# Five V tiles of a decode attention kernel are loaded by four transfers each instead of one

## The chip, the core and the metric

The kernel runs on one core of a Trainium2 chip. The metric is the device time of one execution in microseconds (us). A core has a TensorE (PE) for matrix products, a VectorE (DVE), a ScalarE (ACT), a GpSimd (POOL), and a SyncE (SP), which here does nothing but wait and issue transfers. Sixteen DMA engines move the data from HBM into the on-chip memory, which has 128 partitions (rows).

## What is computed

Four attention layers in a row, each for a single query token: layers 0 and 2 use the weights and caches A, layers 1 and 3 use B. Each layer has 32 heads of 192 dimensions and a cache of 8192 positions, so that every layer reads 32 x 8192 x 192 bf16 values of K and as many of V (about 100 MB each) and does very little arithmetic on each.

```python
q = (layernorm(x) @ wq).reshape(32 heads, 192)
scores = einsum("hd,hkd->hk", q, k_cache) * 192 ** -0.5
p = softmax(scores)
o = einsum("hk,hkd->hd", p, v_cache)
x = x + o.reshape(1, 32 * 192) @ wo
...
x = x + A(x); x = x + B(x); x = x + A(x); x = x + B(x)
```

## The kernel before

**Tiles.** A layer works on 16 pairs of heads. The K cache of a pair, and its V cache, is one tile of 128 partitions by 24576 bf16 values, 49152 bytes in each partition, 6144 KB in all: partitions 0 to 63 hold the first head, 64 to 127 the second, and one partition holds 128 positions of 192 values. Half a tile is TS = 12288 values a partition. The on-chip buffer `pool` has NSLOT = 8 half-tile slots, so that four whole tiles fit at a time.

**Work on a pair.** `products` (line 600) has DVE multiply the K tile in place with the query; PE then adds up over the dimensions by matrix products with an identity (lines 613 and 58) into the score banks S. `softmax` makes the weights p_sb (line 637). `values` (lines 679 and 58) has PE multiply p_sb with the V tile into OY, and `gather` (lines 703, 705, 717) puts the parts together. After five pairs, `project` (line 537) applies a third of the output weights.

**The order of the loads.** The list `plan` holds all loads in the order in which SP issues them: the query weights, then K and V of one pair after another, with the three parts of the output weights between. `allot` gives every load its slots and notes in `before` which earlier holders of these slots must be done. `ahead` issues from the list as long as the release of those holders is already known in the program; in `transfer` SP waits for these events (`*free`) and then issues the load. SP issues in order, so a load that waits for its slot holds back all later ones.

**How a load is issued.** `whole(kind, l, p)` tells whether a tile comes by one transfer. Then `transfer` issues one transfer of 128 partitions for both halves (line 378), and the request for the second half gives back the same event. The other tiles come as two halves (line 380). Every transfer adds 16 to the semaphore semS[i] of its first slot when it has landed, and the event that `SP.op` gives back is the count after it, so that whoever waits for the event waits for all transfers issued on that semaphore so far.

```python
if whole(*n[:3]):
    if n[3] == 1:
        return landed[n[:3] + (0,)]
    f = lambda s: s.dma_start(pool[:, i * TS:(i + 2) * TS], r)
```

Here n is (kind, layer, pair, half), and r is the pair's cache in HBM as 128 rows of 24576 values.

Of the kernel before, what the change touches and what calls it, by code (L numbers as in the profile page):

```python
# [63 lines left out]
PAIRS_W = 5  # L64
NSLOT = 8
KEPT = {0: {("k", 0)}, 1: {("v", 14), ("v", 15)}}


def build(nc, A_x, A_k, A_v, A_wq, A_wo, B_x, B_k, B_v, B_wq, B_wo, out):
    _, H, SK, DH = A_k.shape  # L70
    D = A_x.shape[-1]
    P = 128
# [12 lines left out]
    TS = JU * DH  # L85
# [11 lines left out]
    with ExitStack() as ctx:  # L97
        def sb(name, shape, dt):
            return ctx.enter_context(nc.sbuf_tensor(name, shape, dt))
# [4 lines left out]
        def sem(name):  # L104
            return ctx.enter_context(nc.semaphore(name))

        ident = sb("ident", [P, P], BF16)
        pool = sb("pool", [P, NSLOT * TS], BF16)
# [61 lines left out]
        SP = Queue()  # L170
        semS = [sem(f"semS{i}") for i in range(NSLOT)]
        semOL, semOE, semOB, semVQ, semX, semOUT = [sem(n) for n in ("semOL", "semOE", "semOB", "semVQ", "semX", "semOUT")]

        e = PO.op(lambda g: g.memset(ident[:], 0.0))
# [6 lines left out]
        e = PO.op(lambda g: g.memset(mask, 0.0))  # L181
        for t in range(G):
            e = PO.op(lambda g, t=t: g.affine_select(
                out=mask, in_=mask, compare_op=ALU.not_equal, fill=1.0,
                base=-32 * t, pattern=[[-1, 2], [-2, VK]], channel_multiplier=1), e)
# [10 lines left out]
        def pair(l, p):  # L196
            return ORDER[l]["pairs"][p]

        def first_load(kind, l, p):

            n = (kind, pair(l, p))
            if l >= 2 and n in KEPT[l - 2]:
                return (l - 2, ORDER[l - 2]["pairs"].index(n[1]))
            return (l, p)

        def stays(kind, l, p):
            return l < 2 and (kind, pair(l, p)) in KEPT[l]

        def whole(kind, l, p):

            if kind == "t":
                return False
            if kind == "k":
                return l < 2 and p not in (PAIRS_W, 2 * PAIRS_W) or l == 3 and p > 1
            if p == NPAIR - 1:
                return False
            return l != 2 or p not in (0, PAIRS_W, 2 * PAIRS_W)
# [7 lines left out]
        for l in range(NL):  # L225
# [8 lines left out]
            for p in range(NPAIR):  # L234
# [17 lines left out]
                if p < NPAIR - 2:  # L252
                    if first_load("v", l, p) == (l, p):
                        plan += [("v", l, p, u) for u in range(2)]
                        if l == 2 and p == 1:
                            i = plan.index(("k", l, 1, 0))
# [76 lines left out]
        def wq_rows(l, g):  # L333

            c0, k = Q_PARTS[g]
            if l < 2:
                i = place[("wq", l, 0)] * TS
                return pool[:, i + c0 * QW:i + (c0 + k) * QW].rearrange("p (c n) -> p c n", c=k)
            return slot[place[("wq", l, g)]][:, 0:k * QC].rearrange("p (c n) -> p c n", c=k)

        def quarters(n):
            return n[0] == "v" and n[2:] == (NPAIR - 1, 1) and NB[n[1]] > 0

        def transfer(n):
            l = n[1]
            o = ORDER[l]
            w = W[l % 2]
            free = [freed[b] for b in before[n]]
            if n[0] in ("wol", "woe"):
                r0 = o["wol"] * PD  # L350
                a, b = (0, OI) if l < 3 else (0, OI - 1) if n[0] == "wol" else (OI - 1, OI)
                return SP.op(lambda s: s.dma_start(
                    rows[:, a * D:b * D], w["wo"][r0:r0 + PD].rearrange("(p i) n -> p (i n)", p=P)[:, a * D:b * D]),
                    *free, sem=semOL if n[0] == "wol" else semOE, inc=16)
            if n[0] == "t":
                return max(free, key=lambda e: e[1]) if free else None
            if n[0] == "wob":
                r0 = o["wo"][2] * PD
                return SP.op(lambda s: s.dma_start(
                    slot[place[("wo", l, 2)]][:, (NW - NB[l]) * D:NW * D],  # L360
                    w["wo"][r0:r0 + PAIRS_W * PD].rearrange("(p i) n -> p (i n)", p=P)[:, (NW - NB[l]) * D:]),
                    sem=semOB, inc=16)
            if n[0] == "vq":
                n = ("v", l, NPAIR - 1, 1)
            i = place[n]
            t = slot[i]
            if n[0] in "kv":
                h = 2 * pair(l, n[2])
                r = w[n[0]][0, h:h + 2].rearrange("h (p j) d -> (h p) (j d)", j=J)
                if quarters(n):  # L370
                    x = TS // 2
                    if n in landed:
                        return SP.op(lambda s: s.dma_start(t[:, x:], r[:, TS + x:]), sem=semVQ, inc=16)
                    return SP.op(lambda s: s.dma_start(t[:, 0:x], r[:, TS:TS + x]), *free, sem=semS[i], inc=16)
                if whole(*n[:3]):
                    if n[3] == 1:
                        return landed[n[:3] + (0,)]
                    f = lambda s: s.dma_start(pool[:, i * TS:(i + 2) * TS], r)
                else:
                    f = lambda s: s.dma_start(t, r[:, n[3] * TS:(n[3] + 1) * TS])  # L380
            elif n[0] == "wq" and l < 2:
                f = lambda s: s.dma_start(pool[:, i * TS:i * TS + DC * QW], w["wq"].rearrange("(p c) n -> p (c n)", c=DC))
            elif n[0] == "wq":
                c0, k = Q_PARTS[n[2]]
                f = lambda s: s.dma_start(
                    wq_rows(l, n[2]),
                    w["wq"][:, o["q1"] * PD:o["q1"] * PD + QC].rearrange("(p c) n -> p c n", c=DC)[:, c0:c0 + k, :])
            else:
                r0 = o["wo"][n[2]] * PD
                k = NW - NB[l] if n[2] == 2 else NW  # L390
                f = lambda s: s.dma_start(
                    t[:, 0:k * D], w["wo"][r0:r0 + PAIRS_W * PD].rearrange("(p i) n -> p (i n)", p=P)[:, 0:k * D])
            return SP.op(f, *free, sem=semS[i], inc=16)

        def need(n):

            while n not in landed:
                m = plan[issued[0]]
                issued[0] += 1
                landed[m] = transfer(m)  # L400
            return landed[n]

        def ahead():

            while issued[0] < len(plan):
                m = plan[issued[0]]
                if any(b not in freed for b in before[m]):
                    return
                issued[0] += 1
                landed[m] = transfer(m)  # L410
# [373 lines left out]
        e = SP.op(lambda s: s.dma_start(out[0, 0].rearrange("(h n) -> h n", h=2), ev_z[0:33:32, :]), ev_true, sem=semOUT, inc=16)  # L784
# [54 lines left out]
```

## Time and profile before

| | |
|---|---|
| median of 3 runs | 1981.34 us (1981.29 to 1982.41) |
| profiled execution, its own time | 1981.74 us |
| its span, first to last instruction | 1979.9 us |
| busy share PE, DVE, ACT | 65%, 61%, 7% |
| moved by the DMA engines | 849.22 MB, mean 429 GB/s over the span |
| transfers of whole V tiles of cache A | 27, 6144 KB each, median 26.7 us from issue to landing |
| instruction packets on queue q8 | 45, 0.74 MB |

The profile is one execution. Its second part cuts the span into 40 equal slices: a digit is the busy share in tenths, the line "DMA" is the mean share of the sixteen DMA engines, and the line "GB/s" what they moved. The third part lists the DMA queues: q1 is what SP issues, q8 and q14 bring instructions to the engines. The fourth part is the chain of waits that ended last, followed back from the end. The sixth part lists transfers by line with their size and the median time from issue to landing. Beside the page, the trace can be asked for the busy times of a stretch, for the waits of an engine, for the pieces of the chain in order of time, and it holds the time of each of the sixteen completions of every transfer (though not which DMA engine sent it) and of each packet.

### The profile page before, as it was taken

Reading aid. Unit: us, or ns where it says so; the run is one execution under the profiler, and the core shown is the slowest. Engines: PE = TensorE matmul, PEld = TensorE weight load, DVE = VectorE, ACT = ScalarE, POOL = GpSimd, SP = SyncE. Lnnn points to the kernel's source line nnn. Section 1 sums busy time; section 2 is a strip of 40 time slices with the busy share of each in tenths; the row PEclk is TensorE's granted clock in tenths of the full one; section 3 lists DMA queues with packets and bytes.
Section 4 is the critical chain, followed back from the end, with each engine's and each line's share of the span. In section 5 each row is a group of like instructions: output and inputs, shape, how many; then the busy total and the mean of one; then the engine's idle time right before and its main releaser. Section 6 shows DMA issues by size and latency. Waiting matters only on the chain.

```text
span 1979.9 us, 13244 instructions
## 1 busy us (share of the span) xinstructions
PE 1285.2 (65%) x8248; PEld 146.3 (7%) x3160; DVE 1202.0 (61%) x872; ACT 139.8 (7%) x462; POOL 4.5 (0%) x23
## 2 busy tenths in 40 slices
PE   3567566666466666665785676675676767656668
PEld 0001001000200100000020010010001001000001
DVE  3567467467166656556755565665764765655756
ACT  0000000000000000000010000000000100000000
POOL 0000000000000000000000000000000000000000
PEclk9777776778587777777887877878877778777779
DMA  9999999999999999999999999999999999999998
GB/s 413 431 435 431 432 430 431 434 435 425 434 435 431 430 432 432 430 436 430 427 409 435 426 428 430 430 430 432 431 427 427 436 431 430 435 432 433 430 432 372
DMA packets 26927, 849.22 MB, mean 429 GB/s; under 512 B 3059, under 2 KB 3189, under 8 KB 3829
## 3 DMA queue, kind: packets, MB, share of 16 engines
q1 hardware_dynamic: 26724, 848.38, 99.7%
q8 instruction: 45, 0.74, 0.2%
q14 instruction: 14, 0.11, 0.0%
q10 hardware_dynamic: 144, 0.00, 0.0%
HBM read 848.36 MB, written 0.00 MB: 428 GB/s over the span
## 4 chain that ended last, share of the span: by engine, by line
DMA 61%; PE 23%; DVE 13%; ACT 1%; issue 1%; SPq 0%
DMA pool<-in_B_k_cache_dram 24%; DMA pool<-in_A_v_cache_dram 19%; DMA pool<-in_A_k_cache_dram 14%; PE S L58 13%; DVE pool L600 10%; PE OY L58 5%; DMA pool<-in_B_v_cache_dram 4%; PE OY L679 3%; ACT p_sb L637 1%; DVE OY L703 1%; DVE s_sb L622 1%; PE S L613 1%; DVE acc L705 1%; PE OY L537 1%; DVE m_bf L624 0%
## 5 line engine op out<-in xcount | busy, mean ns | idle before, releaser
L600 DVE TENSOR_TENSOR pool<-pool,q_sb 128x3072 bf16<-128x3072 bf16 (+1 forms) x368 | 851.0, 2378 | 191.2 <-DMA pool<-in_B_k_cache_dram 106.5
L58 PE MATMUL S<-pool,ident 128*128 128x512 bf16 x2944 | 784.0, 426 | 15.5 <-DVE pool L600 14.5
L703 DVE TENSOR_TENSOR OY<-OY,small 128x1536 f32<-128x1536 f32 x60 | 106.0, 1766 | 250.6 <-PE OY L58 250.5
L717 PE MATMUL TB<-acc,small 128*1 128x192 f32 x240 | 82.9, 496 | 210.2 <-DVE acc L705 210.2
L613 PE MATMUL S<-pool,ident 128*128 128x512 bf16 x128 | 62.1, 485 | 216.5 <-DVE pool L600 216.3
L58 PE MATMUL OY<-pool,p_sb 128*16 128x512 bf16 x1920 | 200.0, 493 | 0.0
L679 PE MATMUL OY<-pool,p_sb 128*16 128x512 bf16 (+1 forms) x1216 | 147.3, 493 | 61.2 <-DMA pool<-in_A_v_cache_dram 57.7
L622 DVE TENSOR_REDUCE s_sb<-S 128x64 f32<-128x512 f32 x128 | 87.8, 686 | 126.1 <-PE S L58 126.0
L705 DVE TENSOR_REDUCE acc<-OY 128x192 f32<-128x1536 f32 x60 | 105.4, 1757 | 2.0
L526 ACT ACTIVATE q_sb<-QM 128x192 bf16<-128x192 f32 x60 | 19.8, 330 | 952.7 <-PE QM L520 952.7
L728 ACT ACTIVATE rows<-TB,small 1x192 bf16<-1x192 f32 x120 | 43.1, 405 | 587.5 <-PE TB L717 587.5
L693 DVE RECIPROCAL small<-TB 1x2 f32<-1x2 f32 x64 | 11.2, 175 | 93.2 <-PE TB L652 75.3
L637 ACT ACTIVATE p_sb<-s_sb,small 64x128 bf16<-64x128 f32 x128 | 55.7, 435 | 159.4 <-DVE small L631 158.6
L613 PEld LDWEIGHTS S<-pool,ident 128*128 128x128 bf16 x128 | 12.9, 101 | 693.3 <-DVE pool L600 574.7
L652 PE MATMUL TB<-small,ones 128*1 128x2 f32 x120 | 11.4, 165 | 74.1 <-ACT p_sb L637 74.1
L679 PEld LDWEIGHTS OY<-pool,p_sb 128*16 128x16 bf16 (+1 forms) x1216 | 38.9, 106 | 212.2 <-issue 141.4
L627 PE MATMUL QM<-ident,m_bf 128*64 128x64 bf16 x128 | 14.1, 217 | 54.4 <-DVE m_bf L624 53.8
L717 PEld LDWEIGHTS TB<-acc,small 128*1 128x1 f32 x240 | 19.8, 102 | 304.5 <-DVE acc L705 277.6
L631 DVE TENSOR_REDUCE small<-QM 128x1 f32<-128x64 f32 x64 | 14.3, 224 | 33.7 <-PE QM L627 33.7
L520 PEld LDWEIGHTS QM<-rows,one_b 1*64 1x64 bf16 x120 | 6.2, 100 | 337.9 <-issue 332.0
L537 PE MATMUL OY<-oT,pool 128*128 128x1 bf16 x675 | 28.6, 178 | 1.9 <-ACT oT L583 1.9
L537 PEld LDWEIGHTS OY<-oT,pool 128*128 128x128 bf16 x675 | 27.8, 131 | 3.8 <-ACT oT L583 2.5
(76 smaller groups left out, 224.2 us busy)
## 6 DMA issues: line engine op xcount, KB each, us to landing
pool<-in_B_k_cache_dram SPq DMA_DIRECT2D x28, 6144.0 KB, 36.7
pool<-in_B_v_cache_dram SPq DMA_DIRECT2D x28, 6144.0 KB, 30.4
pool<-in_A_v_cache_dram SPq DMA_DIRECT2D x27, 6144.0 KB, 26.7
pool<-in_A_k_cache_dram SPq DMA_DIRECT2D x34, 3072.0 KB, 20.4
pool<-in_A_k_cache_dram SPq DMA_DIRECT2D x14, 6144.0 KB, 35.8
pool<-in_A_v_cache_dram SPq DMA_DIRECT2D x10, 3072.0 KB, 14.5
pool<-in_B_k_cache_dram SPq DMA_DIRECT2D x8, 3072.0 KB, 21.5
pool<-in_A_wo_dram SPq DMA_DIRECT2D x6, 2400.0 KB, 21.7
```

The lines of the kernel that those rows point to most:

```text
L58: return t.add_instruction(mybir.InstMatmult(name=t.bass.get_next_instruction_name(), engine=mybir.EngineType.PE, ins=[t.lower_ap(rhs), t. ...
L526: lambda a: a.activation(q_sb[i][:], QM[:, 0:DH], ACT.Copy), e, last["q"][i], bank=QMu)
L537: e = PE.op(lambda t, i=i, c=c, f=y_first[0], fin=n[0] == "wol" and i == k - 1: t.matmul(YB[:, c:c + 1], lhsT=t3[:, i, c:D:DC], rhs=o[:, i ...
L600: e = DV.op(lambda v, d0=d0: v.tensor_tensor(k3[:, :, d0:d0 + QD], kin[:, :, d0:d0 + QD], q_sb[qi][:, d0:d0 + QD].unsqueeze(1).broadcast_t ...
L613: t.matmul(S[:, :], lhsT=ident[:], rhs=k3[:, :, d0:d0 + R], start=True, stop=fin) if d0 == 0 else
L622: lambda v, u=u: v.tensor_reduce(s[:, u * JU:(u + 1) * JU], SP_[u][:].rearrange("p (j r) -> p j r", r=R), AX.X, ALU.add), ev_S[p, u], last ...
L637: ev_p[p] = AC.op(lambda a, h=h, r=r: a.activation(p_sb[par][r, :, h], s[r, :], ACT.Exp, bias=negm[par][r, 0:1], accum_out=l_col[par][r, h ...
L679: t.matmul(o, lhsT=x, rhs=y, start=f, stop=fin) if c == 0 else
L703: e = DV.op(lambda v: v.tensor_tensor(o3, o3, pick[:, 0:VK].unsqueeze(2).broadcast_to([P, VK, DH]), ALU.mult), bank=Ou)
L705: e = DV.op(lambda v: v.tensor_reduce(acc[:], O.rearrange("p (i d) -> p d i", d=DH), AX.X, ALU.add), e, bank=Ou)
L717: e = PE.op(lambda t, h=h: t.matmul(TB[96:97, C_O + h * DH:C_O + (h + 1) * DH], lhsT=half[:, h:h + 1], rhs=acc[:], start=True, stop=True), ...
L728: last["TO"] = last["row_written"] = AC.op(lambda a, h=h: a.activation(orow[:, o0 + h * DH:o0 + (h + 1) * DH], TB[96:97, C_O + h * DH:C_O ...
```

## The change

A table SHARED names five V tiles, four in layer 0 (pairs 6, 7, 8 and 9) and one in layer 2 (pair 6). Each of these is loaded by four transfers instead of one, all on the same semaphore:

1. partitions 0 to 111, all columns;
2. partitions 112 to 127, the first columns;
3. the first `a` partitions from 112 on, the last columns;
4. the remaining partitions up to 127, the last columns.

For pair 6 of layer 0, `a` is 8 and the last columns are 18432 values (36864 bytes), so that transfers 3 and 4 have 8 partitions each; for pair 6 of layer 2 they have 8 partitions and 12288 values (24576 bytes). For pairs 7, 8 and 9 of layer 0 the last columns are 2048 values (4096 bytes), and transfers 3 and 4 have 4 and 12, 2 and 14, 6 and 10 partitions. The data that lands is the same. The event given back is that of the fourth transfer, hence the count after all four. By the words that describe the change, transfers of 8 partitions run on the lower eight DMA engines instead of all sixteen, and the three tiles with small pieces mark which engine is which. On the other engines (PE, DVE, ACT, POOL) no instruction is added, removed or moved; SP issues 15 transfers more.

```diff
 KEPT = {0: {("k", 0)}, 1: {("v", 14), ("v", 15)}}
+SHARED = {("v", 0, 6): (8, 18432), ("v", 0, 7): (4, 2048), ("v", 0, 8): (2, 2048), ("v", 0, 9): (6, 2048),
+          ("v", 2, 6): (8, 12288)}
...
                     if n[3] == 1:
                         return landed[n[:3] + (0,)]
+                    if n[:3] in SHARED:
+                        a, x = SHARED[n[:3]]
+                        x = 2 * TS - x
+                        for c0, c1, p0, p1 in ((0, 2 * TS, 0, P - 16), (0, x, P - 16, P),
+                                               (x, 2 * TS, P - 16, P - 16 + a), (x, 2 * TS, P - 16 + a, P)):
+                            e = SP.op(lambda s, c0=c0, c1=c1, p0=p0, p1=p1: s.dma_start(
+                                pool[p0:p1, i * TS + c0:i * TS + c1], r[p0:p1, c0:c1]), *free, sem=semS[i], inc=16)
+                        return e
                     f = lambda s: s.dma_start(pool[:, i * TS:(i + 2) * TS], r)
```

## The prediction

> **What bounds the kernel.** I read the slices first, then the queues, then the chain of waits, then the stretch in which the four tiles of layer 0 arrive.
>
> ```profile
> span 1979.9 us, 13244 instructions
> ...
> DMA  9999999999999999999999999999999999999998
> GB/s 413 431 435 431 432 430 431 434 435 425 434 435 431 430 432 432 430 436 430 427 409 435 426 428 430 430 430 432 431 427 427 436 431 430 435 432 433 430 432 372
> ...
> q1 hardware_dynamic: 26724, 848.38, 99.7%
> q8 instruction: 45, 0.74, 0.2%
> ...
> DMA 61%; PE 23%; DVE 13%; ACT 1%; issue 1%; SPq 0%
> ```
>
> The DMA engines are busy from the first slice to the last at 425 to 436 GB/s, with three weaker ones (start, the passage from layer 1 to 2, end). The next lines are the stretch around the four tiles: busy time and number of instructions of PE, weight loads, DVE, ACT and POOL, then granted clock, DMA share, GB/s; then the chain of waits in it (start, duration); then SP's waits over the whole run (total, times, longest).
>
> ```profile
> 218.00:320.00 102.00, 63.93 (x358) 4.03 (x86) 69.76 (x38) 6.09 (x21) 0.00 (x0) 0.76 1.00 430
> ```
>
> ```profile
> 208.88 38.68 DMA pool<-in_A_k_cache_dram
> ...
> 270.94 34.75 DMA pool<-in_A_k_cache_dram
> ```
>
> ```profile
> SPq L49 <- PE S L58: 733.1, 34, 26.6
> SPq L378 <- PE OY L58: 407.6, 49, 21.5
> ```
>
> DMA share 1.00 beside PE at 63% and DVE at 68% of the stretch: the arithmetic waits for the stream. The chain's pieces last 35 to 39 us although a tile takes 14.53 us from one landing to the next: a load lies some 20 us behind earlier ones. V of pair 6 of layer 0 is issued at 198.90 and has landed at 233.02, 34.1 us later. SP waits long for free slots, yet the stream doesn't run dry. So whatever makes the stream longer makes the kernel longer, one for one, and SP's time is covered.
>
> The sixteen completions of each transfer show a finer thing. They don't come together: the last trails the first by 2.7 us at the four tiles, by 5.3 us in the last V transfer of layer 1 and by 4.7 us at the end, and a tile is there only when the last one is. The instruction packets of q8 make much of this: the lag grows from 3.1 to 4.7 us across the one at 1766.0. Followed through the trace, these steps of about 1.55 us fall in turn on eight of the sixteen engines; which eight, no row tells.
>
> **The rate.** A whole tile gives each engine 393,216 bytes in 14.53 us: 27.06 GB/s. But in every cache tile each engine also serves eight rows of its own. So 27.06 GB/s can be the limit of an engine or the limit of eight rows, and this trace can't tell: no cache load of less than 128 partitions is in it. The whole forecast hangs on that.
>
> **Part 1, the last sixteen rows.** If the engine limits, the pieces cost by bytes per engine. Pair 6 of layer 0 gives engines 0 to 7 12,288 + 2 x 36,864 bytes = 3.18 us instead of 49,152 = 1.82 us: +1.36 us, and the others -1.36 us. In layer 2 it is +0.91 and -0.91 us. The mark tiles move 4,096 bytes (0.15 us) a time, 0.45 us at most together. If the rows limit, sixteen neighbouring rows draw on between two groups (all neighbours share) and sixteen (no two share). I take four, an estimate between these ends, since the rows that share need not all be neighbours. Then the sixteen rows get 4 x 27.06 = 108.2 GB/s, and an 8-row piece, whose rows touch two groups, 54.1. Mark tiles: 16 x 45,056 bytes in 6.66 us where they had 1.66: +5.0 us, three times, 15.0. Pair 6 of layer 0: 1.82 us for the first columns, and two pieces of 294,912 bytes at 5.45 us one after the other on the same eight engines, 12.7 - 1.82 = +10.9 us. Layer 2: 3.63 + 2 x 3.63 - 1.82 = +9.1 us. Sum 35.0 us. With two groups the same working gives 35.0 + 23.6 + 20.0 = 78.6, with eight 13.1.
>
> [...]
>
> **Part 2, the 112 rows.** Seven rows an engine, 344,064 bytes: 12.71 us if the engine limits, as now. If rows limit, sixteen engines stand on 112 / 8 = 14 groups, so that at every moment at least two groups serve two engines; four of sixteen engines go at half speed, each about a quarter of the time: 12.71 / 4 = 3.2 us a tile, 15.9 us for five. Ends: 0 and 63.6 (always two to a group).
>
> **Part 3, fifteen more transfers.** Two half tiles take 2 x 7.30 = 14.60 us where a whole takes 14.53, so 0.07 us each: 1.05 us of stream. On SP each costs some 0.33 us of issue, about 1 us a tile, behind which the next K load is issued later; that is hidden by the 20 us of queue. If the cover were gone, it would be 5 us. No wait is added: the three further transfers find the same slots free. PE, queued behind its wait for V, waits for all four.
>
> **What is not won back.** Engines 0 to 7 carry the slow pieces and always have queued work behind them, so their delay stays to the layer's end. The others run ahead and then wait for slots.
>
> **Sum.** 35.0 + 15.9 + 1.05 = 52.0 us. The profiled execution took 1981.74 us (span 1979.9 and 1.8 around it), 0.4 over the median: 1981.74 + 52.0 - 0.4 = 2033 us.
>
> **Rivals.** (a) The engine limits and the eight engines that get the instruction packets are the upper ones. Then the latest engines are relieved by 1.36 us before the passage to layer 2 and by 0.91 us before the end: -2.27 + 1.05 = -1.2 us, 1980.1. For it speaks that the lag is real (4.7 us at the end) and that both ends wait for the last engine; against it, that nothing says that these are the upper eight. Not slower, and decided at the first tile: if V of pair 6 lands less than 2 us late. Even a perfect levelling wins no more: the latest engine is some 2.8 and 2.4 us behind the mean at the two ends, 5.2 - 1.05 = 4.1 us, 1977.2. (b) The engine limits and the latest engines are among the lower eight: +1.36 + 0.91 + 1.05 = +3.3 us, 0.45 more by the marks, 1984.7 to 1985.1. (c) The 8-row pieces run on all sixteen engines after all: bytes stay even, only part 3 is left, 1982.4. (d) Lags pile up: engines that are tens of us apart meet others' rows in ordinary tiles also, and with two groups (95.5 us, 2076) that goes beyond 2080.
>
> **How the numbers follow.** Rows limit: 0.58, from 2003 (eight groups, 13.1 + 8 + 1) to 2076 (two groups), this case's own range. I hold it likelier since each engine's rows are always its own in the loads here, an arrangement that makes sense if sharing costs. (a) 0.14, (b) 0.16, (c) 0.05, (d) 0.07. The range of 1980 to 2080 leaves out (d) and about half of (a). About 0.2%, 4 us, is what a measurement of this kernel can tell from no change. Faster by that is only the far end of (a): 0.03. Within it are the rest of (a), nearly all of (b), and (c): 0.31. Slower: 0.66.
>
> **What would show it.** Right: V of pairs 6 to 9 of layer 0 and of pair 6 of layer 2 land later than the loads ahead of them explain, the whole tile after 20 us or more instead of 14.53; their packets last longer than the 1815 ns of a 49,152-byte packet; GB/s falls in slices 5 to 7 (198 to 346 us) and in 25 (1188 to 1237 us), and nowhere else; the sixteen completions lie 10 us and more apart; PE's wait for in_A_v grows. Part 1 alone: packets of the 112 rows keep 1815 ns and those of rows 112 to 127 don't. Part 3: SP's added issues are all shorter than 0.5 us. Wrong: all packets keep their rate, GB/s stays at 430 there, and the lag of the last completion changes by one or two us only; then the engine is the limit, and (a), (b) or (c) holds.

## The result, and the profile after

The changed kernel takes 2102.73 us (median of 6 executions, 2091.77 to 2103.74) beside 1981.74 us for the kernel before (median of 6, 1981.29 to 1983.5): a ratio of 1.0594 with a 95% interval from 1.0569 to 1.0619. It is 121 us slower. The forecast was 2033 us, 52 us slower, with a range up to 2080: right in direction and in kind, much too small in size. The profiled execution took 2103.51 us, 121.8 more than the profiled one of before.

First the page of the kernel after: the span, the DMA share and the rate in 40 slices of 52.5 us, the queue on which SP issues, and the shares of the chain that ended last.

```profile
span 2101.7 us, 13259 instructions
...
DMA  9999999999999999999999999999999999999998
GB/s 414 433 433 431 246 237 239 225 428 427 430 399 433 433 433 430 433 430 433 433 420 405 425 434 421 297 432 413 435 425 425 435 433 433 433 433 428 432 433 370
...
q1 hardware_dynamic: 26964, 848.38, 99.4%
...
DMA 59%; PE 22%; DVE 13%; another core or an unknown queue 5%; ACT 1%; issue 1%; SPq 0%
```

The bytes on q1 are the same, 848.38 MB. The DMA engines read as busy as before in every slice, but in slices 5 to 8 (210 to 420 us) they move 225 to 246 GB/s where they moved 430, and in slice 26 (1313 to 1366 us) 297. These are the places of the four tiles of layer 0 and of the one of layer 2, as forecast; elsewhere the rate is the old one. The share counts the time with a packet under way, not the bytes: between 218 and 320 us it reads 1.01 at 241 GB/s, before 1.00 at 430. The share line alone would show nothing.

The same in one stretch of the kernel after (busy time and number of instructions of PE, weight loads, DVE, ACT and POOL, then granted clock, DMA share, GB/s):

```profile
218.00:320.00 102.00, 38.16 (x210) 2.51 (x55) 37.34 (x22) 3.34 (x12) 0.00 (x0) 0.63 1.01 241
```

Between 218 and 320 us PE works 38.16 us instead of 63.93 and DVE 37.34 instead of 69.76. They idle because the stream is slow. The chain of waits of the kernel after in this stretch (start, duration, what) names the place:

```profile
240.71 16.61 another core or an unknown queue
257.36 0.60 PE OY L689 x4
...
295.45 15.79 another core or an unknown queue
311.28 0.60 PE OY L689 x4
```

Here the chain waits about 16 us before the first product with each of the two V tiles. The trace cannot say which of the four transfers on one semaphore came last, so it writes "unknown queue"; line 689 is the product of p_sb with V (679 before). The waits over the whole run (total, times, longest) put them down to the V and K tiles of cache A all the same; before, PE's wait for V was 57.7 us with a longest of 9.7, DVE's for K 83.2 and 9.8:

```profile
PE OY L689 <- DMA pool<-in_A_v_cache_dram: 139.6, 23, 20.1
```

```profile
DVE pool L610 <- DMA pool<-in_A_k_cache_dram: 125.3, 28, 15.3
```

SP's added issues are as cheap as forecast. Its timeline after (start, duration, number of issues joined) has four issues in 1.5 us, where one issue of a whole tile takes some 0.33 us:

```profile
199.02 1.54 SPq L385 DMA_DIRECT2D pool<-in_A_v_cache_dram  x4
```

Comparing when each tile's last completion comes, after against before, the delay grows at the five V tiles and at the K tiles between them: V of pairs 6, 7, 8 and 9 of layer 0 adds 21.5, 20.5, 19.7 and 18.6 us, and the K tiles of pairs 6 to 9 ahead of them 2.8, 4.3, 5.5 and 9.3, which makes 102.2 in all. The delay then stays within some 2 us, until in layer 2 K and V of pair 6 add 2.6 and 17.2. At the end it is 121.7: nothing is lost anywhere else and nothing is won back.

Packets, worked out from the trace: one of 49,152 bytes takes mostly 1815 to 1828 ns in ordinary stretches, as before. Of those that begin from 225 to 250 us the middle half takes 3.1 to 3.8 us, and the slowest 8.2. Of the pieces in layer 0, the 36,864-byte packets take 5.5 us (median) where the bytes alone would take 1.36, the 45,056-byte ones 5.38 for 1.66. Each of the eight packets of one 8-row piece of pair 6 begins where one of the other ends (the first 238.69 + 5.11 = 243.80 us, the last 247.93 + 4.95 = 252.88): both pieces run on the same eight engines. That these are the lower ones by number, no row shows; "the lower eight" stands below for the engines that carry an 8-row load, taken to be the same for any eight rows.

### The profile page after: what moved, and what is told of

It reads as the page before. It is cut to its first block, busy times and chain, and to the rows that moved or that the text cites. A ratio compares the mean times of both kernels' runs of the same rounds, so it can differ in the third digit from the quotient of the medians.

```text
span 2101.7 us, 13259 instructions
## 1 busy us (share of the span) xinstructions
PE 1282.1 (61%) x8248; PEld 145.7 (7%) x3160; DVE 1202.3 (57%) x872; ACT 139.8 (7%) x462; POOL 4.5 (0%) x23
## 3 DMA queue, kind: packets, MB, share of 16 engines
q1 hardware_dynamic: 26964, 848.38, 99.4%
## 4 chain that ended last, share of the span: by engine, by line
DMA 59%; PE 22%; DVE 13%; another core or an unknown queue 5%; ACT 1%; issue 1%; SPq 0%
DMA pool<-in_B_k_cache_dram 25%; DMA pool<-in_A_v_cache_dram 19%; PE S L58 13%; DMA pool<-in_A_k_cache_dram 11%; DVE pool L610 10%; PE OY L58 4%; DMA pool<-in_B_v_cache_dram 4%; PE OY L689 3%; ACT p_sb L647 1%; DVE OY L713 1%; PE S L623 1%; DVE acc L715 1%; DVE s_sb L632 1%; PE OY L547 1%
## 5 line engine op out<-in xcount | busy, mean ns | idle before, releaser
L58 PE MATMUL OY<-pool,p_sb 128*16 128x512 bf16 x1920 | 195.3, 484 | 0.0
L727 PEld LDWEIGHTS TB<-acc,small 128*1 128x1 f32 x240 | 19.7, 101 | 304.6 <-DVE acc L715 277.5
```

Of the source, the lines that this page charges most:

```text
L58: return t.add_instruction(mybir.InstMatmult(name=t.bass.get_next_instruction_name(), engine=mybir.EngineType.PE, ins=[t.lower_ap(rhs), t. ...
L727: e = PE.op(lambda t, h=h: t.matmul(TB[96:97, C_O + h * DH:C_O + (h + 1) * DH], lhsT=half[:, h:h + 1], rhs=acc[:], start=True, stop=True), ...
```

## The experiments

### The shapes of the transfers by themselves (e1_shapes)

The theory behind the forecast is that a group of rows has a rate limit of its own. Its rivals: it is the cache's rows in HBM that collide, or a short transfer costs by what it leaves to each DMA engine. This kernel leaves the attention out and returns its input; it only loads cache rows into `pool`, with each load issued when the former has landed, and three bunches of loads at the end.

```diff
+go(lambda s: s.dma_start(pool[0:112, 0:N], a[256:368]))  # 112 rows
+go(lambda s: s.dma_start(pool[0:112, 0:N], a[0:336:3]))  # 112 rows, every third row of the source
...
+go(lambda s: s.dma_start(pool[112:120, 0:N], a[448:456]))  # 8 rows from 112 on
+go(lambda s: s.dma_start(pool[112:120, 0:N], a[448:472:3]))  # 8 rows from 112 on, every third row of the source
+go(lambda s: s.dma_start(pool[0:32:4, 0:N], a[448:456]))  # 8 rows, every fourth
```

> Leaves the whole attention out and returns the input x: a list of loads alone, each issued when the one before has landed (the last eight in three bunches). A packet of one row (49152 bytes) takes 1.82 us when nothing is shared; fixed cost of one load about 2 us. Theory ROWS (rows of a group share 27 GB/s, a group being four neighbouring rows and the four 32 further on, so 16 groups): 128 rows 16.5 us; 112 rows 20 to 28; 64 neighbouring rows (8 groups) about 16.5, the same as 128; 32 neighbouring rows 9, every fourth row 5.6; 16 neighbouring rows (4 groups) 9.3, every fourth and every eighth row 5.6; 8 neighbouring rows (2 groups) 9.3, every fourth row 3.8, every eighth and every sixteenth 5.6; 4 neighbouring rows 9.3, every fourth 3.8; 1 row 3.8. Taking every third row of the source changes nothing. Theory SOURCE (the addresses read in HBM collide): the target rows change nothing, but every third row of the source does, so 8 rows from 112 on differ from 8 rows from 112 on with every third source row, and 8 neighbouring rows equal 8 rows every fourth. Theory ENGINE (an engine's bytes alone count): 128 rows 16.5, 112 rows 14.7, 96 rows 12.9, 64 rows 9.3, 32 rows 5.6, and 16, 8, 4 and 1 rows 3.8 each, whichever rows they are. In the bunches, ROWS where only the engines that meet slow down: during the 8 neighbouring rows the upper eight engines go on at 1.82 us a packet; ROWS where one crowded group holds up all engines: their packets take 7 us too.

SP's timeline of e1_shapes; the time of a load, and from L111 on of a bunch, is from its first issue to the first of the next one:

```profile
2.48 0.35 SPq L86 DMA_DIRECT2D pool<-in_A_v_cache_dram  x1
20.18 0.33 SPq L87 DMA_DIRECT2D pool<-in_A_v_cache_dram  x1
...
54.92 0.34 SPq L89 DMA_DIRECT2D pool<-in_A_v_cache_dram  x1
79.40 0.32 SPq L90 DMA_DIRECT2D pool<-in_A_v_cache_dram  x1
103.51 0.31 SPq L91 DMA_DIRECT2D pool<-in_A_v_cache_dram  x1
...
153.51 0.53 SPq L93 DMA_DIRECT2D pool<-in_A_v_cache_dram  x1
171.50 0.47 SPq L94 DMA_DIRECT2D pool<-in_A_v_cache_dram  x1
189.49 0.49 SPq L95 DMA_DIRECT2D pool<-in_A_v_cache_dram  x1
199.96 0.32 SPq L96 DMA_DIRECT2D pool<-in_A_v_cache_dram  x1
...
257.26 0.28 SPq L103 DMA_DIRECT2D pool<-in_A_v_cache_dram  x1
266.21 0.27 SPq L104 DMA_DIRECT2D pool<-in_A_v_cache_dram  x1
274.94 0.71 SPq L105 DMA_DIRECT2D pool<-in_A_v_cache_dram  x1
279.44 0.59 SPq L106 DMA_DIRECT2D pool<-in_A_v_cache_dram  x1
285.48 0.56 SPq L107 DMA_DIRECT2D pool<-in_A_v_cache_dram  x1
291.64 0.25 SPq L108 DMA_DIRECT2D pool<-in_A_v_cache_dram  x1
300.24 0.64 SPq L109 DMA_DIRECT2D pool<-in_A_v_cache_dram  x1
304.90 0.23 SPq L110 DMA_DIRECT2D pool<-in_A_v_cache_dram  x1
308.44 0.35 SPq L111 DMA_DIRECT2D pool<-in_B_v_cache_dram  x1
...
347.25 0.35 SPq L114 DMA_DIRECT2D pool<-in_B_v_cache_dram  x1
...
380.55 0.33 SPq L117 DMA_DIRECT2D pool<-in_B_v_cache_dram  x1
...
412.35 0.33 SPq L119 DMA_DIRECT2D pool<-in_B_v_cache_dram  x1
```

128 rows take 17.70 us (L86), yet 112 rows take 24.48 (L89): seven eighths of the bytes, 6.8 us more. Taking every third row of the source changes this little: 112 rows take 24.11 (L90), and 8 rows from 112 on 8.73 (L104) beside 8.95 (L103). So a collision of neighbouring cache rows in HBM is not the cause. 64 neighbouring rows take 17.99 (L93), as long as 128; every second row of the 128, with the same bytes, 10.47 (L95). Eight neighbouring rows take 8.95, every fourth of 32 takes 4.50 (L105), though each row is one packet on one engine in both (each load adds eight completions, one by one). So neither the engine nor the number of rows decides, but which rows they are.

Other loads of the same kernel give the size of a group. One row takes 3.54 us; 4 neighbours take 8.60, 8 take 9.02, 16 take 9.60, 32 take 9.89. From each I take the fixed part, 3.54 less the 1.82 us of a 49,152-byte packet, 1.72. Four rows then need 6.88 us, nearly four packets' time (7.28): four neighbours share one group's rate. Every fourth of 16 rows, also four, takes 4.66 us (L109). Sixteen rows get 786,432 bytes / 7.88 us = 100 GB/s, 3.7 times 27.06: four groups. 32 and 64 rows get 192 and 193 GB/s, 7.1 times 27.06: the second 32 rows bring no new groups. The rows that share are not all neighbours: of 8 rows, every fourth of 32 takes 4.50 us, but every eighth of 64 6.04 (L106) and every sixteenth of 128 6.16 (L107), so that rows 32 or more apart share too, as theory ROWS had it (3.8, 5.6 and 5.6); exactly which rows they are, these loads do not tell.

Of the bunches, a tile of 128 rows, 8 neighbouring rows and another tile take 38.8 us (L111); with 8 rows of every fourth 33.3 (L114); without them 31.8 (L117). And behind the 8 neighbouring rows the sixteen completions of the last tile lie only 2.5 us apart, though only half of the engines had a piece. The packets show it directly: the sixteen that begin between 324.5 and 325.2 us, by their number one on each engine, all take 4.7 to 6.7 us instead of 1.82. The other half was held up as well.

### One transfer for the last sixteen rows (e2_two_parts)

```diff
-for c0, c1, p0, p1 in ((0, 2 * TS, 0, P - 16), (0, x, P - 16, P),
-                       (x, 2 * TS, P - 16, P - 16 + a), (x, 2 * TS, P - 16 + a, P)):
+for c0, c1, p0, p1 in ((0, 2 * TS, 0, P - 16), (0, 2 * TS, P - 16, P)):
```

> The five tiles by two transfers instead of four: 112 rows and 16 rows, all columns, so that no transfer has fewer than 16 rows. ROWS with one crowded group holding up all: the 112 rows cost as in the changed kernel (about 22 to 25 us instead of 12.7) and the 16 rows 7.3 us instead of 1.8, so each tile costs 14 to 18 us more than before: 2050 to 2070 us in all. The forecast as recorded: 3.2 + 5.5 us a tile, 2025. ENGINE: 1982.

It took 2068.68 us (one execution), 86.6 above the kernel before (1982.07). The page's rate line of e2_two_parts:

```profile
GB/s 411 439 429 434 264 294 272 325 434 431 429 433 432 431 434 429 435 431 430 436 408 408 427 430 387 341 435 423 432 429 429 436 428 435 430 433 431 432 434 371
```

Without any 8-row piece and with no engine given more than another, about seven tenths of the loss is there, in the same slices. The split of the rows costs by itself, and more than the 2025 us that the forecast's terms give.

### Four transfers that cut the columns (e3_columns)

```diff
-for c0, c1, p0, p1 in ((0, 2 * TS, 0, P - 16), (0, x, P - 16, P),
-                       (x, 2 * TS, P - 16, P - 16 + a), (x, 2 * TS, P - 16 + a, P)):
+for c0, c1, p0, p1 in [(j * TS // 2, (j + 1) * TS // 2, 0, P) for j in range(4)]:
```

> The five tiles by four transfers each, as many as in the changed kernel, but each of all 128 rows and a quarter of the columns. All theories in which rows or engines are shared: only the 15 further transfers are left, 15 x 0.07 = 1.05 us: 1982.5 to 1983.5. If it were the number of transfers or their smaller size that costs, it would be near the changed kernel's 2102.

1982.97 us (median of 11) beside 1982.07 (15): a ratio of 1.0005, from 0.9996 to 1.0014. Fifteen transfers more cost 0.9 us where 1.05 was forecast, and the interval does not exclude zero. Neither the number nor the smaller size of the transfers is the cause.

### Which engines are late (e4_which_eight)

The kernel before, with a load of 8 rows (every fourth of 32) by 16 bytes into a spare tile behind eight of the V tiles, so that the completions of the engines that carry an 8-row load, the lower eight, can be told apart.

```diff
+e = SP.op(f, *free, sem=semS[i], inc=16)
+marked[0] = SP.op(lambda s: s.dma_start(mk[0:32:4, c:c + 8], r[0:32:4, 0:8]), sem=semMK, inc=16)
```

> The kernel before with eight more loads of 8 rows (every fourth row from 0 to 28) by 16 bytes into a tile that nobody reads, behind V tiles in the four layers: their eight completions tell where the engines that carry 8-row loads stand among the sixteen completions of the tile before. Time 1981.5 to 1982.5 us in every theory. Rival (a): the eight completions are the early ones, the instruction packets go to the other eight. Rival (b): they are among the late ones. Neither: four and four.

It took 1981.44 us (one execution). At the marked tile near the end of layer 1 the sixteen completions come at 0, 0.1, 0.3, 0.3, 1.0, 1.2, 1.4, 3.1, 3.4, 3.6, 3.7, 4.1, 4.5, 4.8, 5.3 and 5.5 us, and the marks of the lower eight, less the 0.18 us by which the first mark trails, come at 0, 0.1, 0.3, 1.0, 1.4, 3.2, 3.5 and 4.9. So the lower eight are neither the early nor the late half: five are among the seven early ones, three among the late. The latest of them is 0.6 us before the very latest engine; at the last marked tile, in layer 3, it is 0.5 us before it. Even with no sharing between rows, the 1.36 us that the change gives the lower eight would put that one at 6.2 us, behind the last engine of the kernel before at 5.5. Rival (a), the only case that would have won anything, had no place to win it; this last step is argued from the offsets, not run.

### The price of each piece in a running stream (e5_bunches)

Again loads alone, the attention left out: a tile of 128 rows, then what is to be priced, then another tile of 128 rows, all queued at once.

```diff
+go(lambda s: s.dma_start(pool[:, 0:N], b[0:128]))
+go(lambda s: s.dma_start(pool[0:112, N:2 * N], b[128:240, 0:N]), False)
+go(lambda s: s.dma_start(pool[112:128, N + 0:N + 6144], b[240:256, 0:6144]), False)
+go(lambda s: s.dma_start(pool[112:120, N + 6144:2 * N], b[240:248, 6144:N]), False)
+go(lambda s: s.dma_start(pool[120:128, N + 6144:2 * N], b[248:256, 6144:N]), False)
+go(lambda s: s.dma_start(pool[:, 2 * N:3 * N], b[256:384]), False)
```

> Again loads alone, the attention left out and the input returned: thirteen bunches. Each is issued at once when the one before has landed: a tile of 128 rows, the load or loads under test, another tile of 128 rows. One bunch with nothing between, one with a third tile of 128 rows (14.5 us more). Time added to the bunch with nothing between. From the loads alone of the run of shapes, less 1.7 us of fixed cost (1 row took 3.54 us for a packet of 1.82): 112 rows 22.8 us; 112 and 16 rows 30.6; as pair 6 of layer 0 (112, 16 by 6144 columns, 8 and 8 rows) 22.8 + 2.0 + 5.5 + 5.5 = 35.8; as pair 7 (112, 16 by 22528 columns, 4 and 12 rows) 22.8 + 6.7 + 0.6 + 0.6 = 30.7; 16 rows 7.8; 4 rows of 4096 bytes 0.6, every fourth row 0.2; even rows and odd rows 14.6; rows 0 to 63 and rows 64 to 127, 30. With engines 0 to 7 made 3.6 us late by two loads of 8 rows of every fourth: if the cost depends on how the engines stand to each other, the 112 and 16 rows cost another sum than in step. HOLD-UP (a crowded group holds up all engines): in each bunch the completions of the last tile stay within 4 us. PAIRS (only those that meet): the completions of the last tile behind the 8 and 8 rows spread by 7 us or more, the upper eight engines being early.

SP's timeline of e5_bunches, the first issue of each bunch; a bunch lasts until the next one's first issue (the last line is the store of the output, which ends the last bunch):

```profile
2.51 0.37 SPq L86 DMA_DIRECT2D pool<-in_B_v_cache_dram  x1
...
48.69 0.33 SPq L89 DMA_DIRECT2D pool<-in_B_v_cache_dram  x1
...
110.03 0.35 SPq L93 DMA_DIRECT2D pool<-in_B_v_cache_dram  x1
...
179.16 0.35 SPq L99 DMA_DIRECT2D pool<-in_B_v_cache_dram  x1
...
241.51 0.35 SPq L105 DMA_DIRECT2D pool<-in_B_v_cache_dram  x1
...
296.84 0.33 SPq L108 DMA_DIRECT2D pool<-in_B_v_cache_dram  x1
...
335.93 0.33 SPq L111 DMA_DIRECT2D pool<-in_B_v_cache_dram  x1
...
367.43 0.33 SPq L113 DMA_DIRECT2D pool<-in_B_v_cache_dram  x1
...
431.23 0.33 SPq L119 DMA_DIRECT2D pool<-in_B_v_cache_dram  x1
...
477.40 0.33 SPq L123 DMA_DIRECT2D pool<-in_B_v_cache_dram  x1
...
539.97 0.33 SPq L127 DMA_DIRECT2D pool<-in_B_v_cache_dram  x1
...
612.55 0.35 SPq L133 DMA_DIRECT2D pool<-in_B_v_cache_dram  x1
...
662.22 0.57 SPq L139 DMA_DIRECT2D out_dram<-x_sb  x1
```

| between the two tiles (line of its first issue) | bunch | against a whole tile |
|---|---|---|
| nothing (L111) | 31.50 | -14.7 |
| a tile of 128 rows (L86) | 46.18 | 0 |
| 112 and 16 rows (L89) | 61.34 | +15.2 |
| the four parts of pair 6 of layer 0 (L93) | 69.13 | +23.0 |
| the four parts of pair 7 (L99) | 62.35 | +16.2 |
| 112 rows alone (L105) | 55.33 | |
| 16 rows alone (L108) | 39.09 | |
| even rows, then odd rows (L119) | 46.17 | 0.0 |
| rows 0 to 63, then 64 to 127 (L123) | 62.57 | +16.4 |
| engines set apart, then 128 rows (L133) | 49.67 | |
| engines set apart, then 112 and 16 rows (L127) | 72.58 | +22.9 against the line above |

The 112 rows alone add 55.33 - 31.50 = 23.8 us where their bytes need 12.7: **+11.1 us**, and the forecast had 3.2. The other parts of pair 6 add 69.13 - 55.33 - 1.82 = +12.0 (forecast 10.9), those of pair 7 62.35 - 55.33 - 1.82 = +5.2 (forecast 5.0). In the last two rows, two loads of 8 rows, every fourth of 32, come beforehand; they are meant to make the lower eight engines 2 x 1.82 = 3.6 us late, an estimate, and make the bunch with a whole tile 3.5 us longer (49.67 against 46.18). The same 112 and 16 rows then cost 22.9 us instead of 15.2. The price of a split depends on how the engines stand to each other. Two more bunches, with 4 rows of 4096 bytes between the tiles, took 31.98 us for neighbouring rows and 31.82 for every fourth. And behind the two 8-row pieces of pair 6 the completions of the last tile lie 3.3 us apart, where 7 us or more were expected if only the engines that meet slow down.

### The same five tiles by even and odd rows (e6_even_odd) and by halves (e7_halves)

Both make two transfers of 64 rows and equal bytes per engine.

```diff
+for p in (slice(0, P, 2), slice(1, P, 2)):
+    e = SP.op(lambda s, p=p: s.dma_start(pool[p, i * TS:(i + 2) * TS], r[p]), *free, sem=semS[i], inc=16)
```

```diff
+for p in (slice(0, P // 2), slice(P // 2, P)):
+    e = SP.op(lambda s, p=p: s.dma_start(pool[p, i * TS:(i + 2) * TS], r[p]), *free, sem=semS[i], inc=16)
```

> The five tiles by two transfers of 64 rows each, all even rows and all odd rows: fewer than 128 rows, but rows of every group in each. ROWS: each transfer finds all 16 groups, as the 64 rows of every second alone (10.47 us for four packets): 1982 us, up to 2 us a tile more at the seams with ordinary tiles, 1992. If fewer than 128 rows cost by themselves: 2030 and more. ENGINE: 1982.

> The five tiles by two transfers of 64 neighbouring rows each, 0 to 63 and 64 to 127. ROWS: each transfer finds 8 of the 16 groups and two engines on each (18.0 us alone, the same as for 128 rows), so a tile takes some 30 us instead of 14.5: 5 x 15.5 = 77 us, 2059 us. ENGINE: 1982, as with even and odd rows.

Even and odd: 1982.08 us (median of 10) beside 1981.9 (13), a ratio of 1.000, from 0.9991 to 1.001. Halves: 2074.61 us (one execution), 92.7 more; the five V tiles land 15.9, 16.0, 15.6, 16.6 and 15.1 us later, each close to the 16.4 of the bunch, and the K tiles ahead of them 1.9 to 4.2, so that the total is 15.6 us above the 2059 us expected. The rate lines, first of e6_even_odd, then of e7_halves:

```profile
GB/s 413 433 434 433 430 431 430 435 434 426 435 434 433 430 428 437 427 434 431 428 412 426 432 430 431 431 430 432 432 430 427 433 433 435 429 431 434 435 430 369
```

```profile
GB/s 415 433 434 430 284 276 263 311 430 434 427 434 436 430 430 431 435 428 434 431 408 406 430 427 385 325 437 416 432 431 428 434 431 432 431 433 433 431 433 376
```

With rows taken alternately the stream runs on at 430 GB/s in slices 5 to 8; with neighbouring rows it falls to 263 to 311. Bytes, number of transfers, rows and slots are the same. What differs is which rows each transfer holds, and by e1 that sets how many engines stand on the same group of rows.

### The tiles of the change apart (e8_no_marks, e9_marks_only), and in another order (e10_marks_first)

Each is the kernel after with another table:

```diff
-SHARED = {("v", 0, 6): (8, 18432), ("v", 0, 7): (4, 2048), ("v", 0, 8): (2, 2048), ("v", 0, 9): (6, 2048),
-          ("v", 2, 6): (8, 12288)}
+SHARED = {("v", 0, 6): (8, 18432), ("v", 2, 6): (8, 12288)}  # e8_no_marks
+SHARED = {("v", 0, 7): (4, 2048), ("v", 0, 8): (2, 2048), ("v", 0, 9): (6, 2048)}  # e9_marks_only
+SHARED = {("v", 0, 6): (4, 2048), ("v", 0, 7): (2, 2048), ("v", 0, 8): (6, 2048), ("v", 0, 9): (8, 18432),
+          ("v", 2, 6): (8, 12288)}  # e10_marks_first
```

> The two tiles with 8-row pieces as in the changed kernel, the three mark tiles loaded whole as before. If the parts add up as the landings of the changed kernel say (28.6 us at pair 6 of layer 0 with the K tile behind it, 19.8 at layer 2): 1982 + 48 = 2030. If the marks cost only because the engines came out of pair 6 far apart, then the marks' share is larger than here shown and this stays near 2030 too, but a kernel of marks alone would be below 2055. The forecast as recorded gives 10.9 + 9.1 + 2 x 3.2 + 0.4 = 26.8: 2008.

> Only the three mark tiles (pairs 7, 8 and 9 of layer 0), the two tiles with 8-row pieces loaded whole. In a bunch by itself a mark tile cost 62.27 - 46.08 = 16.2 us more than a whole one, three of them 48.6; in the changed kernel they came on top of the other two by 2102.7 - 2024.1 = 78.6. If they are dear only behind pair 6: 1982 + 49 = 2031, up to 2040 with the engines' ordinary distance of 2.7 us. If crowded tiles in a row make each other dearer, whatever the first one is: 2045 to 2060.

> The same five kinds of tile in another order: the three marks at pairs 6, 7 and 8 of layer 0, the tile with two 8-row pieces of 18432 columns last, at pair 9; layer 2 unchanged. If the 8-row tile is what sets the engines apart and makes the marks behind it dear: 1982 + 3 x 17 + 25 + 19.5 = 2078. If it is the row of crowded tiles itself: as the changed kernel, 2095 to 2105.

The two tiles with 8-row pieces alone took 2024.07 us: the stream ends 42.2 us later than in the trace of before. The three mark tiles alone took 2031.38, 49.6 later, 16.5 a tile as in the bunch. Together that makes 91.8; the profiled execution of the kernel after has 121.7, so about 30 us come on top where both stand in a row. Rate lines, first e8_no_marks, then e9_marks_only, then e10_marks_first:

```profile
GB/s 412 430 432 434 263 421 427 434 435 429 432 434 432 428 434 432 430 433 434 425 401 428 429 430 302 418 426 425 432 433 422 434 435 433 432 430 431 434 433 359
```

```profile
GB/s 417 432 432 429 398 271 280 359 432 431 434 430 433 433 431 432 431 432 433 432 416 424 433 424 434 431 428 433 431 429 423 436 433 432 433 433 428 433 433 368
```

```profile
GB/s 418 428 436 430 273 273 254 260 434 435 427 432 434 433 428 436 430 428 434 432 420 409 428 430 396 302 432 417 432 432 428 432 435 431 429 436 428 435 434 371
```

In the mark tiles' slices the marks alone run at 271 to 280 GB/s; behind the 8-row tile, in the kernel after, at 225 to 239. With the marks first and the 8-row tile last, the kernel took 2084.58 us (one execution; the delay at the end is 102.8 us), 11.0 above the sum of the parts instead of 29.9. That lies between the two expectations, nearer to the 2078 of the theory that the 8-row tile sets the engines apart and so makes the splits behind it dearer. But the landings don't bear this theory out. By the third mark tile e10 is 60.2 us late and e9 49.6, so that 10.6 of the 11.0 us come ahead of the 8-row tile. Behind the 8-row tile, in the kernel after, the marks add 77.9 us (from 24.3 to 102.2). The order seems to matter, but the same three marks, with nothing split before them, differ by 10.6 us as well between pairs 6 to 8 (e10) and pairs 7 to 9 (e9). And two of the six executions of the kernel after took only 2091.77 and 2094.2 us, by which the extra would be 18 to 30; the spread of e8, e9 and e10, one execution each, isn't known.

## Why the prediction was wrong in size

**What bounds the kernel: right.** The delay at the five tiles, 121.7 us, is the delay at the end, one for one.

**The rate: right that the rows limit.** Rivals (a), (b) and (c) fell at the first tile: V of pair 6 lands 24.3 us late, not under 2. The rate of a group of rows is the engine's to within what the loads show (100 GB/s for four groups against 4 x 27.06), so that a whole tile, eight rows an engine at 27.06 GB/s, does not show it. Rows limit had 0.58, with a trace before that has no cache load of fewer than 128 partitions.

**Part 1, the last sixteen rows: right.** Forecast +10.9, three times +5.0, and +9.1, sum 35.0. The bunches give +12.0 and +5.2. For layer 2, e8's K and V land 2.0 + 17.5 us later, which less 11.1 for its 112 rows leaves +8.4. Sum 12.0 + 15.6 + 8.4 = 36.0. The estimate of four groups was right: in e1 sixteen rows got 100 GB/s, 3.7 times 27.06.

**Part 2, the 112 rows: the step that failed.** 3.2 us a tile were forecast and 11.1 are measured, 55.5 instead of 15.9 for five: 39.6 of the missing 69 us. The runs contradict two things in "four of sixteen engines go at half speed, each about a quarter of the time". It took the groups as fourteen of eight neighbours, while Part 1 had just taken four groups for sixteen rows; by e1 a group is four neighbours (8.60 us for the four) and rows 32 or more further off (8 rows, every eighth of 64, 6.04 us where every fourth of 32 took 4.50). And it charged only those engines that meet. In e1 all sixteen packets took 4.7 to 6.7 us beside 8 neighbouring rows. In the kernel after, the 49,152-byte packets of the whole stretch lengthen together, to 3.1 to 3.8 us, and beside the 8-row pieces packets of the K tile behind them take up to 8.2 us, more than four times 1.82. The longest of these begin at 239 to 241 us and so come from engines that have no piece, since the others still work on theirs; of the ten that begin between 240 and 250 us the shortest takes 5.5. So in these runs a crowded group slows all sixteen engines. How much of the missing 7.9 us a tile each of the two makes is argued, not shown: if the 112 rows put two engines on most groups, sharing alone would come near the price, as the forecast's own end of 12.7 us a tile (63.6 for five) says.

**Part 3, fifteen more transfers: right.** 1.05 forecast, 0.9 measured by e3, whose interval includes both zero and 1.05; four issues take 1.5 us of SP and don't show.

**What is not won back: right in the sum, wrong in the picture.** The delay stays. But the other eight engines do not simply run ahead: behind 8 neighbouring rows in e1 all sixteen completions are within 2.5 us.

**Rival (d), lags pile up, given 0.07: the second part of the error, its cause open.** In step, the terms make 36.0 + 55.5 + 0.9 = 92.4 us, and e8 and e9 together have 91.8. The kernel after has some 30 us more (18 by its shortest executions). That lags make this extra is argued, not shown. For it speaks that the completions of the K tiles between the splits do spread, by 10.3, 11.8 and 17.5 us, and that in e5 two 8-row loads ahead (estimated to set the engines 3.6 us apart) raise a split's price from 15.2 to 22.9. Against it, the K tiles of e2 spread by 5.5, 8.1 and 9.9 us, and yet each split behind them adds less than the one before (17.6, 17.2 and 15.1 us after 20.5, K and V together). And some 11 us of extra come without any 8-row piece: e2 has 86.6 us where five times the bunch's 15.2 makes 76, e7 92.7 where five times 16.4 makes 82. The forecast had seen that engines tens of microseconds apart meet others' rows, but priced it by Part 1 with two groups.

**The range.** Its upper end was Part 1 with two groups and Part 2 at its middle value. Part 2's own upper end, 63.6, beside the middle of Part 1, gives 35.0 + 63.6 + 1.05 = 99.7, or 2081: the end that was written down for the term was left out of the range, and what splits in a row add stood outside it.

Three things stay open. How the engines hold one another up (where along the path from HBM to the rows) wasn't tried. What makes splits in a row cost more than the sum of their prices isn't settled. And which rows each engine takes of 112 or of 96 is not in the trace, so that 11.1 us is a measured price and not a derived one.

No run was faster than the kernel before: with even and odd rows it is equal, and since by e1 a group of rows has no more rate than an engine (100 GB/s for four groups against 108.2 for four engines), giving bytes to other engines should win nothing by this way of splitting; no run tried it with rows that don't meet.

## What to carry to other kernels

In a stream bound by DMA, split a tile by columns or by alternate rows, which cost nothing measurable here (ratios of 1.0005 and 1.000), and not by runs of neighbouring rows: 112 + 16 rows cost 15.2 us more than the same 6 MB as 128 rows, two halves 16.4 us. When a shared resource is crowded, price it as if every engine slowed, as here (4.7 to 6.7 us a packet on all sixteen instead of 1.82), until a run shows that only those who meet do. And when several such transfers follow one another, don't rely on the sum of their single prices, and add the terms' own upper ends when drawing the range.

## What the runs showed of the hardware that was not expected

- Fewer rows can take longer: 112 rows 24.48 us and 96 rows 24.57 us, 128 rows 17.70 us, each alone.
- The whole of the 64 even rows takes 10.47 us, 64 neighbouring ones 17.99 us.
- While 8 neighbouring rows are loaded, the packets of the engines without a piece slow too (4.7 to 6.7 us for all sixteen, 1.82 otherwise). In the kernel after the DMA share reads 1.01 while the split tiles come, at 241 GB/s.
- The engines that lag near the end of layer 1 in e4 are of both halves: five of the lower eight are among the seven early completions, three among the late ones.
- Two of six executions of the kernel after are some 10 us shorter than the other four (2091.77 and 2094.2 against 2102.56 to 2103.74), while the kernel before stays within 2.2 us. The cause is not known.
